# A spectral filter kernel on one core: the last matrix is loaded behind the gate's first product, with a new written-out order

## The chip, the cores and the metric

The kernel runs on one core of a Trainium2 chip. The metric is the device time of one execution in microseconds (us), the median of several runs. One execution was also recorded by the hardware profiler; all rows of the profile come from that one, and its times count from the start of its span.

## The reference

Two spectral filters act on the same input `x` (2048 rows of 1024 numbers, bf16), and a gate mixes them:

```python
g = sigmoid((x * gate_w).sum(-1, keepdims=True))      # one number a row
def filt(w_r, w_i):                                   # the same for A and for B
    X = rfft2(x.astype(float32), axes=(-2, -1))       # 2048 x 513
    return irfft2(X * (w_r + 1j * w_i), s=(2048, 1024)).astype(bfloat16)
return g * filt(A_w_r, A_w_i) + (1 - g) * filt(B_w_r, B_w_i)
```

The reference reads `A_x` for both filters. The forward transform is therefore done once.

## The kernel before, in words

All transforms are matrix products with constant matrices, in these steps.

- **Fold and S1.** `x` comes in eight loads on SyncE's (SP's) queue. VectorE folds each (`fS`, `fT`, `f2`), TensorE multiplies with the matrix F (S1), and ScalarE or VectorE evicts from PSUM (Z). A row of the gate's sum is formed on the way (`gate`, `zrow`, `zg`).
- **D and S2.** The transform along a row (D, evicted as Q) and the rest of the transform along the column (S2 and S25, evicted as X and X5), in four quarters sq = 0 to 3.
- **Products.** VectorE multiplies the spectrum with the weights of filter b (0 or 1): four products for every (b, sq), each 128x2052. The weights come in 26 pieces on GpSimd's (POOL's) queue, two transfers each.
- **I1(b, sq, th).** The first part of the inverse along the column, 16 pieces in all, each of 64 matmuls into two PSUM halves. Each half is evicted to a buffer in RING (V, on ScalarE or VectorE), and a DMA writes that buffer to other partitions of TV (the *turn*). The turn of the first half is issued by SP, that of the second by POOL. The buffer is free again when its turn has landed.
- **The gate in the inverse.** The gate's product (`gm`, half 0 and half 1) with the matrix RM and the sigmoid (`sig`) give the gate of each row. VectorE then forms RA = RM * g and RB = RM - RA (`RA`, `RB`, for each half).
- **S1A, S1B, S1H.** The second part of the inverse along the column, with RA for filter A and RB for filter B, so that the mix is made in the same sum. It is evicted as G.
- **Di.** The inverse along a row with the matrix DI, evicted as o. VectorE unfolds it (`u`, `e`, `y0`, `y1`), and SP stores it.

All matmuls are issued from one line, L392; VectorE's elementwise work from L395; evictions on ScalarE from L417 and on VectorE from L418; transfers from L426; the sigmoid from L736. In the profile's tile names R is the spectrum's buffer and later G's; WAB holds `x`, then the weights and products, and in the tail o and e; FM holds the gate and later RA; RM later holds RB.

The order of the work is not found at run time. Every step is a node with the engines that can do it, what it reads and what it writes. Three strings name the order of all 447 nodes (`ORDER`, two digits in base 36 for a node), the engine of each (`ENGS`: p, a, d, g and s for TensorE, ScalarE, VectorE, POOL and SP) and the place of each buffer in RING and PSUM (`CELLS`). Each engine runs its nodes in that order. Before a node it waits on semaphores for what the node reads, and for the last readers of what it overwrites. An engine that waits holds up everything behind it in its own list.

The list of SP in the old order is: the loads of `x` and F, the matrices DM and SK, then RM and DI, both of which wait until the last weight has landed, then SP's half of 16 turns, then nine stores. POOL has the weights and then its half of the 16 turns.

Lines that the change touches or that its steps use:

```python
    def cload(eng, t, off, key, a, b, keys, more=(), **kw):            # a constant matrix
        dma("c_" + key, eng, lambda: [(ap(t, off, [[1, b - a]]).bitcast(dt.uint16), cst[key].ap()[:, a:b])],
            (b - a) * 256e-6, 400, list(more), keys, **kw)
...
    cload("sp", RM, 0, "RM", 0, 2048, ["RM"], more=wk[1])
    cload("sp", DI, 0, "DI", 0, 2048, ["DI"], more=wk[1])
```

`more` is what the load waits for, over what its buffer needs; `wk[1]` are the weights of filter B. The buffer of DI is used for nothing else.

Of the kernel before, what the change touches and what calls it, by code (L numbers as in the profile page):

```python
# [20 lines left out]
PAIRS = {"warm": 12, "S2": 8, "I1": 64, "I1W": 32, "S25": 8, "gate": 8, "zg": 4, "gm": 8}  # L21
DEPTH = ((0, 2), (2, 4), (4, 6), (6, 8), (8, 10), (10, 12), (12, 14), (14, 16))
ORDER = (
    "020b0h030c000i04010506070m0j080n090f0a0g0d0q0s0e0o0t0r0k0y0u0p0z0w0l24150v14100x251b16111a26181g171h1c27191o1e1p1d28121r"
    "1f1q2w29131x1u1s1j2a1v2z1w1t1i2b1y1m301k1z2c2x1n1l22202d232y2132312e333v2f3z3w412g403x422h463y4a472i35434c4b36482j344d44"
    "494e2k4539624f2l4g3a643d2m4h633b3e2n4i653c3n2o3h4j373i3o3f2p4t3g383j3r4u4p2q3s3t4q3p3u2r4k3k3q5o3l2s4z4l3m535p2t504r4m5q"
    "4v544n4o4w4s5e5a5f4x6g5b516i4y665r522u2v6j6b6955676h6a566c685c6e575d6d5g7m6f5s5h6w585t7n595u6p6x5v6u5w5x6s7o6q6t6v606r6k"
    "5y7p615z6y7a6l6n806m6o7v826z7181707y7273837w7b84787x7z76748g7787757q8e858879865k8f7r5l8h7s7c7t5m5i7u8i7d5n5j7e7f8l8j7g8n"
    "8m8k8x8q8o8r7h8p8s7i7k8y8t8z7j9q7l8u9u9r909v8v9s918w9w9t9389929x94959e8a9z999y9f8c8b9a9ga5a18d9ba09ha6a99i9ca2aaa7969dab"
    "a397aoa8a49k98ak9jacapbeal9laqbfad9mamarae9nbganafba9obhatax9pbbasb1agayaubcb2ahazavbdaib3awb0biajc1bjb4bnbkc3b5c2c6b6bo"  # L30
    "c4bpblbqc5b7bsbmbrc9b8btc7bub9bwbvcbbxc8bycabzccc0cdce")
ENGS = (
    "sadsadpsasssdasdsasaspdspdapdpadpagdadpagdpadgpdadpgadpdagpdadpgadppdgapdadgdpapdgadappgdpappgapgpapgdpagpdpagpdpadpgpap"
    "dpgapdagpadpgadpagpdapgdappdpgpaddpdpgapdpagpdadpgpadpdgapddpapdadppapdapdapdassdpadadgpaspdaaspdgpadpadaspdadgpadagdasp"
    "adgspdaadsgpdaadsagpdadpdsgaadgaspdagdspdaadspaddgpaddsdadgpgspadgpspadppaspgapapdppdapadpdaddpadpdpdspapdgadpdpapdapdap"
    "ddpasdspdadpadpaddpaddpadpdadpsadpdadpadpdadpsadspdapdadapdapadpadpsaddaadsdddddddddsds")
CELLS = (
    "07150927d4002940h204097d24069024632094604620042690h460460204620460304h20614062042602355072460024206460248062424608062244"
    "0606a2804226046804202460464206402400684242000464240846c020042284044gk208402008424476508428a02")


def bf16_bits(a):
# [309 lines left out]
def bass_gated_mix__spectral_gfnet__spectral_gfnet__prompt_kernel(  # L352
# [6 lines left out]
    def sb(name, n, dty=BF):  # L359
        t = nc.alloc_sbuf_tensor(name, [128, n], dty)  # L360
        pit[id(t)] = n
        return t

    def ap(t, off, dims, p0=0, np_=128):
        return AP(t, p0 * pit[id(t)] + off, [[pit[id(t)], np_]] + [list(d) for d in dims])
# [6 lines left out]
    DI = sb("DI", 2048)  # L372
# [11 lines left out]
    P = Plan({"ps": 8, "ring": NCELL, "late": 32},  # L384
             {"ps": ("ps", 4), "p1": ("ps", 8), "st": ("ring", 4), "q": ("ring", 2), "qx": ("ring", 2), "v": ("ring", 14),
              "o": ("late", 8), "e": ("late", 8), "y": ("ring", 5), "u": ("ring", 5), "w": ("ring", 1), "dm": ("ring", 1)})
# [4 lines left out]
    def mm(o, l, r, start, stop):  # L391
        return lambda e: e.matmul(o, l, r, start=start, stop=stop, skip_group_check=True)  # L392

    def tt(o, a, b, op):
        return lambda e: e.tensor_tensor(out=o, in0=a, in1=b, op=op)  # L395
# [5 lines left out]
    def vt(n):  # L401
        return {"dve": (0.07 + 0.00052 * n, 0.205 + 0.00052 * n)}

    def pe(name, ns, build, reads, writes, alloc=(), **kw):
        return P.add(name, cost(ns), lambda e: build(), reads, writes, alloc=alloc, **kw)
# [15 lines left out]
    def dma(name, eng, pairs, mb, rate, reads, writes, kind=True, n=1, **kw):  # L421
        if not isinstance(eng, str):
            es = {"pool": (0.6, mb / 118 * 1000), "sp": (0.63, mb / 118 * 1000)}
        else:
            es = {eng: (0.6 * n, mb / rate * 1000)}
        n = P.add(name, es, lambda e: [lambda q, d=d, s=s: q.dma_start(d, s) for d, s in pairs()], reads, writes, dma=kind, **kw)  # L426
        n.mb = mb
        return n

    def psl(t, off, dims, p0=0, np_=128):  # L430
        return ap(PS, t.at * 512 + off, dims, p0, np_)
# [6 lines left out]
    def cload(eng, t, off, key, a, b, keys, more=(), **kw):  # L438
        dma("c_" + key, eng, lambda: [(ap(t, off, [[1, b - a]]).bitcast(dt.uint16), cst[key].ap()[:, a:b])],
            (b - a) * 256e-6, 400, list(more), keys, **kw)  # L440
# [30 lines left out]
    wk = {0: [], 1: []}  # L471
# [104 lines left out]
                wload("W%d%d%d" % (b, c, h), (c, 4 + h), "pool", [rows(b, c, 64 * J, 1, 8 * h, 16 * J + 8 * h, [[64 * NS, 8], [512 * NS, 4], [1, 8 * NS]]) for J in (1, 0)], 0.525, b)  # L576
                wk[b].append(("W", b, c, 4 + h))
    cload("sp", RM, 0, "RM", 0, 2048, ["RM"], more=wk[1])
    cload("sp", DI, 0, "DI", 0, 2048, ["DI"], more=wk[1])
    for c in range(4):  # L580
        gate_row(c)
    P.key = ("gate", 4)
# [145 lines left out]
    for c in range(2):  # L728
        P.key = ("gm", c)
        t = Tile("p1", 2)  # L730
        f = ap(FM, c * 1024, [[1, 1024]])
        rm = ap(RM, c * 1024, [[1, 1024]])
        pe("gm", [128] * 8, lambda c=c, t=t: [mm(psl(t, i * 128, [[1, 128]]), ap(ZG, 8 * c + i, [[0, 128]]),
                                                 ap(RM, (8 * c + i) * 128, [[1, 128]]), True, True) for i in range(8)],
           ["ZG", "RM"], [(t,)], alloc=[t])
        P.add("sig", {"act": (0.92, 1.12)}, lambda e, f=f, t=t: [lambda e: e.activation(f, psl(t, 0, [[1, 1024]]), ACT.Sigmoid)],  # L736
              [(t,)], [("gr", c)], after=[("zrow", i) for i in range(4)])
        P.add("RA", vt(1024), lambda e, f=f, rm=rm: [tt(f, rm, f, ALU.mult)], ["RM", ("gr", c)], [("RA", c)], after=[("gr", c)])
        P.add("RB", vt(1024), lambda e, f=f, rm=rm, c=c: [tt(rm, rm, f, ALU.subtract)],
              ["RM", ("RA", c)], [("RB", c)])  # L740

    for b in range(2):
        for sq in range(4):
# [136 lines left out]
```

## Time and profile before

| what | value |
|---|---|
| median of 3 runs | 122.72 us (122.67 to 123.09) |
| the profiled execution, its time | 122.33 us |
| its span, first to last instruction | 120.5 us |
| granted TensorE clock | 0.993 |
| busy: TensorE, VectorE, ScalarE, POOL | 104.1, 100.2, 96.1, 39.0 us |
| DMA: HBM read, written | 15.01 MB, 4.19 MB |

A row of a timeline or of the chain begins with its start and its duration. "x3" is three instructions merged into one row. What stands in brackets is the idle time of the engine before the row, and what ended it. PE is TensorE, PEld its weight loads, DVE VectorE, ACT ScalarE; a letter q behind an engine is its queue of issues. In a row of transfers the last number is the median time from issue to landing.

The stages, by the rows of the engines: the loads, fold and S1 run to about 22.5, D and S2 to 46, I1 with its turns from 46 to 86, and the tail (S1A to the stores) from 86 to the end, with the last I1 piece at 91.

### The profile page before, as it was taken

Reading aid. Unit: us, or ns where it says so; the run is one execution under the profiler, and the core shown is the slowest. Engines: PE = TensorE matmul, PEld = TensorE weight load, DVE = VectorE, ACT = ScalarE, POOL = GpSimd, SP = SyncE. Lnnn points to the kernel's source line nnn. Section 1 sums busy time; section 2 is a strip of 40 time slices with the busy share of each in tenths; the row PEclk is TensorE's granted clock in tenths of the full one; section 3 lists DMA queues with packets and bytes.
Section 4 is the critical chain, followed back from the end, with each engine's and each line's share of the span. In section 5 each row is a group of like instructions: output and inputs, shape, how many; then the busy total and the mean of one; then the engine's idle time right before and its main releaser. Section 6 shows DMA issues by size and latency. Waiting matters only on the chain.

```text
span 120.5 us, 4292 instructions
## 1 busy us (share of the span) xinstructions
PE 104.1 (86%) x1908; PEld 71.3 (59%) x1908; DVE 100.2 (83%) x137; ACT 96.1 (80%) x110; POOL 39.0 (32%) x72
## 2 busy tenths in 40 slices
PE   6999996899999999895997778978899999999800
PEld 2368855676974865342362334534696999999500
DVE  0459999478988999996999999784449999999991
ACT  4389999668989999957985889933578899999930
POOL 0005999999999400110311131131010100000000
PEclk9999999999999999999999999999999999999997
DMA  3999999999996883892699669979750237145384
GB/s 81 385 423 412 405 278 271 287 358 361 278 260 202 324 330 113 298 254 56 169 258 228 165 193 244 232 207 245 197 160 0 55 124 299 54 174 204 150 348 174
DMA packets 10884, 27.89 MB, mean 231 GB/s; under 512 B 3409, under 2 KB 3409, under 8 KB 10354
## 3 DMA queue, kind: packets, MB, share of 16 engines
q1 hardware_dynamic: 5472, 14.98, 37.4%
q0 software_dynamic: 5248, 12.62, 35.3%
q8 instruction: 15, 0.25, 1.0%
q10 hardware_dynamic: 146, 0.02, 0.1%
q14 instruction: 3, 0.02, 0.1%
HBM read 15.01 MB, written 4.19 MB: 159 GB/s over the span
## 4 chain that ended last, share of the span: by engine, by line
PE 37%; DMA 24%; ACT 17%; DVE 15%; issue 3%; SPq 1%; DVEq 0%; ACTq 0%
PE PS L392 37%; DMA TV<-RING 20%; DVE RING L395 12%; ACT WAB L417 6%; ACT RING L417 5%; DMA WAB<-in_A_x_dram 5%; ACT R L417 4%; DVE WAB L395 3%; DVE RING L418 1%; ACT TV L417 1%; SPq L426 1%; DVEq L251 0%; ACTq L251 0%
## 5 line engine op out<-in xcount | busy, mean ns | idle before, releaser
L417 ACT ACTIVATE RING<-PS 128x1024 bf16<-128x1024 f32 x40 | 39.1, 1028 | 12.7 <-PE PS L392 8.8
L395 DVE TENSOR_TENSOR RING<-WAB 128x1024 bf16<-128x1024 bf16 (+1 forms) x42 | 23.8, 608 | 5.3 <-DMA WAB<-in_A_x_dram 5.0
L395 DVE TENSOR_TENSOR WAB<-R,WAB 128x2052 bf16<-128x2052 bf16 x24 | 28.0, 1224 | 0.2 <-PE PS L392 0.2
L392 PE MATMUL PS<-WAB,SK 64*32 64x512 bf16 x768 | 24.4, 377 | 3.6 <-ACT RING L417 2.1
L417 ACT ACTIVATE R<-PS 128x1024 bf16<-128x1024 f32 (+2 forms) x28 | 23.7, 932 | 1.5 <-PE PS L392 1.5
L426 POOL DMA_DIRECT2D TV<-RING x16 | 8.5, 532 | 47.0 <-ACT RING L417 31.6
L392 PEld LDWEIGHTS PS<-WAB,SK 64*32 64x32 bf16 x768 | 11.0, 92 | 14.3 <-ACT RING L417 4.4
L392 PE MATMUL PS<-RING,TV 128*128 128x256 bf16 x128 | 15.1, 274 | 0.3 <-ACT TV L417 0.3
L417 ACT ACTIVATE WAB<-PS 128x1024 bf16<-128x1024 f32 (+1 forms) x17 | 14.8, 986 | 0.8 <-PE PS L392 0.7
L418 DVE CAST RING<-PS 128x1024 bf16<-128x1024 f32 x8 | 9.8, 1222 | 6.0 <-PE PS L392 3.0
L392 PEld LDWEIGHTS PS<-RING,TV 128*128 128x128 bf16 x128 | 13.5, 114 | 1.3 <-ACT R L417 0.8
L392 PE MATMUL PS<-RM,TV 128*128 128x128 bf16 x128 | 13.3, 219 | 0.5 <-DMA TV<-RING 0.5
L417 ACT ACTIVATE TV<-PS 128x1024 bf16<-128x1024 f32 x14 | 13.3, 1039 | 0.6 <-PE PS L392 0.6
L392 PE MATMUL PS<-FM,TV 128*128 128x128 bf16 x128 | 13.7, 220 | 0.0
L392 PE MATMUL PS<-DI,R 128*128 128x256 bf16 (+1 forms) x128 | 13.4, 259 | 0.2 <-ACT R L417 0.2
L392 PEld LDWEIGHTS PS<-FM,TV 128*128 128x128 bf16 x128 | 12.6, 114 | 1.3 <-DVE RING L418 0.4
L392 PE MATMUL PS<-TV,RING 128*128 128x256 bf16 (+1 forms) x128 | 12.3, 253 | 1.2 <-DVE RING L395 0.8
L392 PEld LDWEIGHTS PS<-RM,TV 128*128 128x128 bf16 x128 | 12.6, 114 | 0.7 <-DMA TV<-RING 0.7
L418 DVE CAST R<-PS 128x1024 bf16<-128x1024 f32 (+2 forms) x11 | 10.1, 935 | 3.4 <-PE PS L392 3.2
L392 PEld LDWEIGHTS PS<-TV,RING 128*128 128x128 bf16 x128 | 10.3, 98 | 4.2 <-DVE RING L395 2.2
L392 PEld LDWEIGHTS PS<-DI,R 128*128 128x128 bf16 x128 | 10.9, 98 | 1.7 <-ACT R L417 0.8
L426 POOL DMA_DIRECT2D WAB<-in_A_w_r_dram x13 | 7.8, 605 | 9.9 <-DMA WAB<-in_A_x_dram 9.9
(41 smaller groups left out, 104.1 us busy)
## 6 DMA issues: line engine op xcount, KB each, us to landing
WAB<-in_A_x_dram SPq DMA_DIRECT2D x8, 512.0 KB, 7.8
TV<-RING POOLq DMA_DIRECT2D x16, 256.0 KB, 4.2
TV<-RING SPq DMA_DIRECT2D x16, 256.0 KB, 4.6
out_dram<-RING SPq DMA_DIRECT2D x7, 512.0 KB, 2.8
WAB<-in_A_w_r_dram POOLq DMA_DIRECT2D x4, 256.5 KB, 5.9
WAB<-in_A_w_i_dram POOLq DMA_DIRECT2D x4, 256.5 KB, 6.2
WAB<-in_B_w_r_dram POOLq DMA_DIRECT2D x4, 256.5 KB, 5.3
WAB<-in_B_w_i_dram POOLq DMA_DIRECT2D x4, 256.5 KB, 5.6
```

What stands on the lines that cost most here:

```text
L392: return lambda e: e.matmul(o, l, r, start=start, stop=stop, skip_group_check=True)
L395: return lambda e: e.tensor_tensor(out=o, in0=a, in1=b, op=op)
L417: return [lambda e: e.activation(o, i, ACT.Copy)]
L418: return [lambda e: e.tensor_copy(o, i)]
L426: n = P.add(name, es, lambda e: [lambda q, d=d, s=s: q.dma_start(d, s) for d, s in pairs()], reads, writes, dma=kind, **kw)
```

## The change

The load of DI is taken from its place beside RM. It now waits for RA of half 0 instead of the weights of filter B, and stands in SP's list between its halves of turn(1,1,0) and turn(1,0,0):

```diff
     cload("sp", RM, 0, "RM", 0, 2048, ["RM"], more=wk[1])
-    cload("sp", DI, 0, "DI", 0, 2048, ["DI"], more=wk[1])
     for c in range(4):
         gate_row(c)
...
         P.add("RB", vt(1024), lambda e, f=f, rm=rm, c=c: [tt(rm, rm, f, ALU.subtract)],
               ["RM", ("RA", c)], [("RB", c)])
+    P.key = ("in", 1)
+    cload("sp", DI, 0, "DI", 0, 2048, ["DI"], more=[("RA", 0)])
```

The three strings are new as well; here are their beginnings:

```diff
 ORDER = (
-    "020b0h030c000i04010506070m0j080n090f0a0g0d0q0s0e0o0t0r0k0y0u0p0z0w0l24150v14100x251b16111a26181g171h1c27191o1e1p1d28121r"
+    "020b0h030c000i04010506070m0j080n090f0a0g0d0q0e0s0o0r0t0k0y0u0p0z0w0l0v241510140x251b18111a12261h19161g13271o1c171j281e1i"
...
 ENGS = (
-    "sadsadpsasssdasdsasaspdspdapdpadpagdadpagdpadgpdadpgadpdagpdadpgadppdgapdadgdpapdgadappgdpappgapgpapgdpagpdpagpdpadpgpap"
+    "sadsadpsasssdasdsasaspsdpadpdpadpaagdpdagdpadgpdapdagpdadgpdadpgadppdagpdadpgapddagpdpapgadpappgpgpapgdpagpdpagpdpapgadp"
...
```

Decoded, the lists differ in this way. Of the I1 pieces, with the engines of their two evictions (A ScalarE, D VectorE), first half before second:

```
old: 010 AA, 011 AD, gm 0, 000 AA, 021 AA, 001 AA, 020 AA, 030 AA, 111 AA, 031 AA, 120 AA, 110 AA, gm 1,
     100 AD, 130 DA, 131 DA, S1A, 101 AD, S1A, S1B ..., 121 AD
new: 010 AA, 011 DA, gm 0, 000 AA, 020 AA, 021 AA, 001 AA, 030 AA, 031 AA, 111 AA, 120 AA, 110 AA, gm 1,
     100 AA, 130 AA, S1A, 131 AD, 101 AA, S1A, S1B ..., 121 AA
```

- Evictions that change engine: 31. ScalarE has 116 nodes instead of 111, VectorE 132 instead of 137.
- The first turn: the old order evicts the second half of V(0,1,0) first, the new one the first half.
- VectorE's last products are followed by RA and RB of half 0 and then of half 1 in the new order; in the old one by RA of half 1, RA of half 0, RB of half 1, RB of half 0.
- In the forward stage the third gate row and its eviction stand ahead of the last S1 pieces (in the old order the eviction stands behind the last Z). The order of the pieces of D and S2 and some of their evictions' engines change.
- Buffers: in the old order an eviction V takes the buffer of the V that stands about five places ahead of it; in the new one five to seven places in the middle and four near V(1,0,0) and V(1,3,0).
- In the tail the pieces 9 to 13 of S1H, G, Di and o come in another order, and so do the stores. The second G of the tail is evicted by VectorE instead of ScalarE, and both evictions of the last I1 piece by ScalarE.

Weights, matrices, matmuls and transfers are the same in number, shape and size.

More of the change, by code (lines that the diff above doesn't have):

```diff
@@ L23 @@
 ORDER = (
-    "020b0h030c000i04010506070m0j080n090f0a0g0d0q0s0e0o0t0r0k0y0u0p0z0w0l24150v14100x251b16111a26181g171h1c27191o1e1p1d28121r"
-    "1f1q2w29131x1u1s1j2a1v2z1w1t1i2b1y1m301k1z2c2x1n1l22202d232y2132312e333v2f3z3w412g403x422h463y4a472i35434c4b36482j344d44"
-    "494e2k4539624f2l4g3a643d2m4h633b3e2n4i653c3n2o3h4j373i3o3f2p4t3g383j3r4u4p2q3s3t4q3p3u2r4k3k3q5o3l2s4z4l3m535p2t504r4m5q"
-    "4v544n4o4w4s5e5a5f4x6g5b516i4y665r522u2v6j6b6955676h6a566c685c6e575d6d5g7m6f5s5h6w585t7n595u6p6x5v6u5w5x6s7o6q6t6v606r6k"
@@ L28 @@
[L28 to L31, printed above, removed]
+    "020b0h030c000i04010506070m0j080n090f0a0g0d0q0e0s0o0r0t0k0y0u0p0z0w0l0v241510140x251b18111a12261h19161g13271o1c171j281e1i"
@@ new lines @@
+    "1d1p2y291f1w1k1m1q1l2a2v1r2z1x1u2b1n1s1z1y1t2c311v222w202d32232x2130332e3y2f3u3z402g3v3w412h453x49462i344a4b35382j4c4243"
+    "39472k443e48623c2l3f4h643d2m3a634i2n3q3b363m3g3r3h2o3n3o3j374f653i2p3p3k4d5o3l4g2q3s4e4y5p2r3t4j4z2s4o4k4s4p522t4t4q4l5q"
+    "534m4u4n4r4v595d5a4w6g5e506i4x666h512u6j6b67545r6968556e6a5b6c565c6f5f6w6d5s5g7m575t6x585u6k7n5v6u5w6p6l7o6n6m6v6s6o5x82"
+    "6q6t6r6y80605y83615z7p7371816z7276707v7874778g7579847y7w8h7z857x7q7a87868e885j7b7t7r8f7u7c5k7s5h5n5i8i7d5l7f5m7e8x8l7g8j"
@@ L32 @@
+    "8m8n8k8o8q8p7h8r8s7k8y8t7i7l9u8u8z7j9q9v909r8v919s8w9w9t9289939x95949e8c9z99969f8a9y8d9a97a99ga08ba59b98aa9ha1a69c9iab9d"
+    "a7a2ac9jax9ka3a8b19ma4ayaoadae9lb2beagapaz9nafbfb3b0bab49obgbbb59pakb6bhahbcalb7aqaibdb8amajarbjb9bnbianc1bkboatbpbqasc2"
+    "bsbrblc4c3aubmc5c6buavbtc7c8awbwc9cbcabvccbxcdbycebzc0")
 ENGS = (
-    "sadsadpsasssdasdsasaspdspdapdpadpagdadpagdpadgpdadpgadpdagpdadpgadppdgapdadgdpapdgadappgdpappgapgpapgdpagpdpagpdpadpgpap"
-    "dpgapdagpadpgadpagpdapgdappdpgpaddpdpgapdpagpdadpgpadpdgapddpapdadppapdapdapdassdpadadgpaspdaaspdgpadpadaspdadgpadagdasp"
@@ L35 @@
-    "adgspdaadsgpdaadsagpdadpdsgaadgaspdagdspdaadspaddgpaddsdadgpgspadgpspadppaspgapapdppdapadpdaddpadpdpdspapdgadpdpapdapdap"
-    "ddpasdspdadpadpaddpaddpadpdadpsadpdadpadpdadpsadspdapdadapdapadpadpsaddaadsdddddddddsds")
+    "sadsadpsasssdasdsasaspsdpadpdpadpaagdpdagdpadpgdapdagdpadgpdadpgadppdagpdadpgapddagpdpapgadpappgpgpapgdpagpdpagpdpapgadp"
+    "dpgapadpgapdagpdagpappddpgapddpdagappdaagpapdgapdgpapdpgapddappaadppapdapdapdasdpaddaspagpdaagpdspadpadaspdadgpadasdagpd"
+    "agspdaadgsdpadagaspdagdsdpaadgaspdasdgpdaadgpasdsdpadadspagagpsadspgpappagpdaspdpapdpapadpdaddpadpdpadgpdpadspdsapdapdpa"
@@ L37 @@
+    "pdadpddapdsapdddapdapddapdpadpadspdadpadpdadpsadspdapdadapdapadpadsapddaadsdddddddddsds")
 CELLS = (
-    "07150927d4002940h204097d24069024632094604620042690h460460204620460304h20614062042602355072460024206460248062424608062244"
-    "0606a2804226046804202460464206402400684242000464240846c020042284044gk208402008424476508428a02")
+    "07150927d4002940h2d4007924h602074260294024702h07402409240700274062h40620506420460202355672042006224460068242a06406248062"
+    "4a240062460240462268a026022046002404680242606040286424002c664008286042c0440208408476c50072846")
```

## The prediction

> **What bounds the kernel now.** I read the page first, then the chain of work that ended last, then busy time by stretches, and then each engine's timeline around the two places that the change touches. Times are microseconds from the start of the span. I call a piece of the inverse I1(b,q,t), its two evictions V(b,q,t) and their two transfers turn(b,q,t), as the kernel does.
>
> ```profile
> span 120.5 us, 4292 instructions
> PE 104.1 (86%) x1908; PEld 71.3 (59%) x1908; DVE 100.2 (83%) x137; ACT 96.1 (80%) x110; POOL 39.0 (32%) x72
> GB/s 81 385 423 412 405 278 271 287 358 361 278 260 202 324 330 113 298 254 56 169 258 228 165 193 244 232 207 245 197 160 0 55 124 299 54 174 204 150 348 174
> PE 37%; DMA 24%; ACT 17%; DVE 15%; issue 3%; SPq 1%; DVEq 0%; ACTq 0%
> ```
>
> Three engines are above 80%, and the chain changes hands between four resources. So no single sum over the span decides; each stage has its own limit.
>
> ```profile
> 22.50:46.00 23.50, 23.43 (x288) 17.39 (x296) 19.42 (x25) 20.53 (x24) 18.07 (x32) 1.00 0.88 291
> 50.00:54.00 4.00, 3.26 (x84) 1.55 (x88) 4.00 (x5) 2.89 (x4) 0.56 (x1) 1.00 0.96 233
> 54.00:57.00 3.00, 1.58 (x48) 0.69 (x56) 2.07 (x3) 2.11 (x3) 0.00 (x0) 1.00 0.24 65
> 70.00:75.00 5.00, 4.11 (x136) 2.01 (x120) 5.00 (x5) 4.30 (x5) 1.49 (x3) 1.00 0.85 217
> 75.00:78.00 3.00, 2.70 (x96) 1.35 (x104) 2.25 (x4) 2.78 (x4) 0.53 (x1) 1.00 1.03 243
> 78.00:82.00 4.00, 3.18 (x109) 1.46 (x94) 3.17 (x5) 1.47 (x3) 1.04 (x2) 1.00 0.78 195
> 99.50:118.00 18.50, 14.65 (x195) 13.14 (x193) 18.27 (x38) 16.12 (x22) 0.00 (x0) 1.00 0.50 200
> ```
>
> The columns are the stretch and its length, busy PE, PEld, DVE, ACT and POOL, the granted clock, the DMA share and GB/s. TensorE fills the forward stage (23.43 of 23.50). VectorE fills 50 to 54, 70 to 75 and the tail. The DMA engines are full at 50 to 54 and 75 to 78, with a hole between (0.24 in 54 to 57), in which TensorE and ScalarE idle too.
>
> ```profile
> 49.25 5.55 DMA TV<-RING
> 61.12 5.43 DMA TV<-RING
> 67.89 3.24 DMA TV<-RING
> 75.27 4.83 DMA TV<-RING
> 81.44 4.50 DMA TV<-RING
> 85.99 10.84 PE PS L392 x200
> ```
>
> These are the turns on the chain: start, time to landing. An eviction can't write a buffer until the turn that reads it has landed, so between 48 and 86 the end runs eviction, turn, eviction. After 86 TensorE leads, then ScalarE and VectorE.
>
> **The inverse matrix leaves its early place.**
>
> ```profile
> 46.04 0.32 SPq L426 DMA_DIRECT2D RM<-c_RM  x1
> 46.41 0.43 SPq L426 DMA_DIRECT2D DI<-c_DI  x1
> RM<-c_RM SPq DMA_DIRECT2D x1, 512.0 KB, 5.4
> DI<-c_DI SPq DMA_DIRECT2D x1, 512.0 KB, 7.2
> TV<-RING POOLq DMA_DIRECT2D x16, 256.0 KB, 4.2
> TV<-RING SPq DMA_DIRECT2D x16, 256.0 KB, 4.6
> 54.89 1.02 ACT L417 ACTIVATE RING<-PS 128x1024 bf16<-128x1024 f32 x1 [1.70 <-DMA TV<-RING]
> 47.93 2.85 ACT L417 ACTIVATE RING<-PS 128x1024 bf16<-128x1024 f32 x3 [0.29 <-PE PS L392]
> 52.95 1.05 PE L392 MATMUL PS<-WAB,SK 64*32 64x512 bf16 x32
> ```
>
> DI lands 7.2 after its issue at 46.41, at 53.6, and lies over the first turn, which takes 5.55 and lands at 54.80. ScalarE idles 1.70 for it and starts V(0,0,0) at 54.89. With DI gone I give the first turn the median of the SP queue, 4.6: the new order evicts its SP half first (47.93 + 1.02), it is issued 0.3 later as now, at 49.25, and lands at 53.85. I1(0,0,0) ends at 52.95 + 1.05 = 54.0 at the latest, so V(0,0,0) starts at 53.9 instead of 54.89: **1.0 gained**. The ends are nothing (RM alone crowds it as much) and the whole 1.70.
>
> The Trainium skill (DMA: Bandwidth & Descriptors, Anatomy of one DMA — SWDGE (gpsimd) path) gives a transfer 2.0 us and its bytes at 436 GB/s, which is 2.6 us for a turn, an estimate; by it all 1.70 would go and the sum below would be 1.6 gained instead of 0.9. The trace does not agree, with 3.24 to 5.55 on its chain, and the measurement decides.
>
> **The forward stage and its new order.** Up to the first I1 nothing is added or removed. TensorE has 0.07 free in 22.5 to 46, so the order can gain nothing there.
>
> ```profile
> 21.33 1.02 ACT L417 ACTIVATE TV<-PS 128x1024 bf16<-128x1024 f32 x1 [0.18 <-PE PS L392]
> 22.25 0.59 ACT L417 ACTIVATE FM<-PS 128x512 bf16<-128x512 f32 x1
> ```
>
> It can lose: a gate row's eviction (0.59, now behind the last eviction of the first transform) moves ahead of it. ScalarE idles 0.18 there, and TensorE does the gate's product earlier too and has it off its list later. I take 0, with ends 0.1 gained and 0.6 lost. Some evictions change places between VectorE and ScalarE, each of which idles over 2.9 in that stretch.
>
> **Does the early gain last to 75?** VectorE multiplies through this stage.
>
> ```profile
> 56.86 1.23 DVE L395 TENSOR_TENSOR TV<-R,WAB 128x2052 bf16<-128x2052 bf16 x1 [0.93 <-ACT R L417]
> 58.01 11.48 DVE L395 TENSOR_TENSOR WAB<-R,WAB 128x2052 bf16<-128x2052 bf16 x10
> 69.64 5.79 DVE L395 TENSOR_TENSOR WAB<-R,WAB 128x2052 bf16<-128x2052 bf16 x5 [0.15 <-PE PS L392]
> 76.19 1.29 DVE L395 TENSOR_TENSOR FM<-RM,FM 128x1024 bf16<-128x1024 bf16 x2 [0.75 <-ACT FM L736]
> ```
>
> The 0.93 at 56.86 waits for the eviction that stands on ScalarE behind V(0,0,0). One us earlier there closes this hole, and the products then run back to back at (11.48 - 1.23) / 9 = 1.14 each; the last one ends at 74.5 instead of 69.64 + 5.79 = 75.4. So VectorE lets 0.9 through and little more (0.93 + 0.15 are all its idle time). The turns must keep pace as well. Counted in the lists, the eviction that reuses a buffer stands on average five places behind the one that filled it in the old order, and six from the 13th to the 21st eviction in the new one. That is room for the middle. I carry **0.9**, and count no more of it as gain.
>
> **The inverse matrix at its new place.** DI waits for RA of half 0, which needs only a gate that is long evicted, so it comes right behind the last product: issue at about 75.3, behind turn(1,1,0) (75.27 on the chain, some 0.9 sooner then) and ahead of SP's half of turn(1,0,0). Queued behind the wait on SP are turn(1,0,0), (1,3,0), (1,3,1), (1,0,1), (1,2,1) and all stores; POOL's halves pass it by. The issue itself costs SP 0.43, which nothing there feels. Its 524 KB at the highest rate of the page, 423 GB/s, take the DMA engines 1.24. Turn(1,0,0) is the one held; its reader is S1B at 85.99, which in any case waits until 85.94 for turn(1,3,0) (81.44 + 4.50), issued behind it. The part that can hurt is the sharing with turn(1,1,0), whose landing releases V(1,3,0). It is issued over 0.5 ahead on the same queue. I take **0.2 lost**; the ends are 0 and 2.5 (1.24 on each of two turns that follow one another on the chain).
>
> ```profile
> L392 PEld LDWEIGHTS PS<-DI,R x128: 96/98/99, 88.7 to 113.9; 128*128 128x128 bf16 x128
> ```
>
> DI is first read at 88.7. With its old 7.2 it lands at 82.5. That cover is 6 us; without it TensorE would stand at the first Di2.
>
> **The last evictions and the tail.**
>
> ```profile
> 85.71 1.23 DVE L418 CAST RING<-PS 128x1024 bf16<-128x1024 f32 x1 [2.61 <-DMA TV<-RING]
> 86.66 2.85 ACT L417 ACTIVATE R<-PS 128x1024 bf16<-128x1024 f32 x3 [0.69 <-PE PS L392]
> 88.90 1.22 DVE L418 CAST R<-PS 128x1024 bf16<-128x1024 f32 x1 [1.96 <-PE PS L392]
> ```
>
> The new order gives both evictions of I1(1,0,1) to ScalarE, ahead of the first G, where VectorE took one: (2.85 - 1.02) / 2 = 0.92 more on ScalarE, of which some 0.5 lie behind the landing of turn(1,3,0). In return the second G goes to VectorE, which idles 1.96 before 88.90, so the third is out 0.9 sooner. From there on both orders give VectorE five evictions and ScalarE loses one; VectorE has 0.23 free from 99.5 to 118. I take **0.2 gained**, between 0.9 either way (one eviction's worth).
>
> **Sum.** -0.9 for the early place, +0.2 for the new one, -0.2 for the tail: -0.9. The profiled execution took 122.33 (span 120.5 and 1.8 around it), so 121.4; the median of the runs is 122.72, 0.39 above it, so **121.8**. The case's own range, with 0 to 1.7 for the first term, is 121.2 to 122.4.
>
> **The rivals.**
>
> *More comes through.* TensorE has holes in the late pieces that end with an eviction that itself waited for a turn.
>
> ```profile
> 72.22 1.93 PE L392 MATMUL PS<-WAB,SK 64*32 64x512 bf16 x64 [0.59 <-ACT RING L417]
> 79.88 1.93 PE L392 MATMUL PS<-WAB,SK 64*32 64x512 bf16 x64 [0.82 <-DVE RING L418]
> ```
>
> If six places of room close these two, 1.4 more: 120.4. For it speaks that one turn on the chain took only 3.24. Against it, the new order's last reuses, before V(1,0,0)'s second half and V(1,3,0), are back at four places.
>
> *Moved, not saved.* The DMA engines give back at 75 what they gained at 47: then the new place costs 1.24 instead of 0.2, and the sum is +0.1, 122.8. For it speaks the share of 1.03 in 75 to 78, higher than the 0.96 of the old place. The same time comes out if the change does not do what it says, because RM and four turns in a row crowd each other without DI.
> The Trainium skill (DMA: Bandwidth & Descriptors, Issuing engines are not separate DMA queues) says that transfers from every issuing engine share the same 16 DMA engines and interleave; this is that rival's rule, and the full shares while both queues are in use agree.
>
> *Slower: a tight loop in front of the matrix.* In the new order V(1,1,0), turn, V(1,3,0), turn, S1B is a chain with four places of room, all on ScalarE's queue in order, and DI falls between the two turns. If both are held by 1.24, the new place costs 2.5, and the sum is +1.4: 124.1. It decides once turn(1,1,0) lands later than 81.4, since 80.10 (75.27 + 4.83) is its landing now and the 0.9 won early, with the tail's 0.2, is then spent. Against it, the share falls to 0.78 in 78 to 82, where the second turn would run.
>
> **How the numbers follow.** Forecast 0.42, more 0.12, moved 0.18, slower 0.28. About 0.5% (0.6 us) is what a measurement of this kernel can tell from no change. Faster by more: three quarters of the forecast's range, nearly all of the first rival and a sliver of the second, 0.45. Slower by more: nearly all of the third rival and the edges of the others, 0.30. The rest, 0.25. The range takes in both ends, 120.3 to 124.1, and leaves out half of the first rival and about a third of the last.
>
> **What would show it.** Right: the first turns land under 5 us and V(0,0,0) starts near 53.9; VectorE's wait of 0.93 is gone and the last product ends near 74.5; DI is issued near 75 and lands before 83; S1B starts near 85. The forecast is wrong if the first turns still take 5.5, if a new wait appears before a product on VectorE, if turn(1,1,0) or turn(1,3,0) takes over 6, or if S1B starts early and the end does not, which would put the fault in the tail.

## The result, and the profile after

The kernel after takes 122.68 us (median of 20 runs, 121.4 to 124.92), the kernel before 121.88 us beside it (20 runs, 120.77 to 123.21). The ratio is 1.0061, with an interval of 1.0035 to 1.0087: slower by 0.6%, where the forecast was 0.9 us faster. The time lies inside the forecast's range of 120.3 to 124.1; its direction is the other one. Ratios here leave out executions more than 1.5% above the fastest of their kernel, so they need not be the ratio of the medians; the profiles of old_order_late, old_order_late_free, new_order_late_free and new_order_half are of such executions, and no price of a change is taken from them.

The profiled execution took 122.99 us. Its page and its chain of work, as far as they answer to the lines shown of before:

```profile
span 121.2 us, 4292 instructions
DMA 32%; POOL 24%; PE 15%; DVE 15%; ACT 7%; issue 3%; SPq 1%; DVEq 0%
...
46.03 5.27 DMA RM<-c_RM
...
60.73 4.97 DMA TV<-RING
...
70.11 4.04 DMA TV<-RING
...
75.23 4.86 DMA TV<-RING
...
81.16 5.59 DMA TV<-RING
...
86.79 11.73 PE PS L392 x216
```

DMA's share of the chain went from 24% to 32%, but not by the turns: theirs fell from 19.5% to 16.1%. Ahead of 51 the chain after runs through POOL's issues of the weights, the last weight and RM (24.3%, 5.0% and 4.3%), where before it ran through VectorE and TensorE. The chain before had TensorE from 85.99 (S1B); now it has it from 86.79. The engines' timelines around the two places, and the row of DI among the transfers:

```profile
53.97 1.02 ACT L417 ACTIVATE RING<-PS 128x1024 bf16<-128x1024 f32 x1 [0.87 <-PE PS L392]
57.42 17.18 DVE L395 TENSOR_TENSOR WAB<-R,WAB 128x2052 bf16<-128x2052 bf16 x15
74.18 1.02 ACT L417 ACTIVATE RING<-PS 128x1024 bf16<-128x1024 f32 x1 [0.27 <-DMA TV<-RING]
75.80 1.57 SPq L426 DMA_DIRECT2D DI<-c_DI  x1
DI<-c_DI SPq DMA_DIRECT2D x1, 512.0 KB, 7.1
TV<-RING SPq DMA_DIRECT2D x16, 256.0 KB, 4.4
80.11 1.93 PE L392 MATMUL PS<-WAB,SK 64*32 64x512 bf16 x64 [1.45 <-ACT RING L417]
86.79 1.08 PE L392 MATMUL PS<-RM,TV 128*128 128x128 bf16 x16 [1.10 <-DMA TV<-RING]
```

What the prediction asked for up to 75 is there: V(0,0,0) starts at 53.97, the products run without a hole and end at 57.42 + 17.18 = 74.60. But V(1,1,0) starts at 74.18, where before had it at 74.22 by its timeline, and from there every step is late. So there are two questions: where the early microsecond went, and what the late load costs.

### The profile page after: what moved, and what is told of

The parts are those of the page before. It is cut to its first block, busy times and chain, and to the rows that moved or that the text cites. A ratio compares the mean times of both kernels' runs of the same rounds, so it can differ in the third digit from the quotient of the medians.

```text
span 121.2 us, 4292 instructions
## 1 busy us (share of the span) xinstructions
PE 104.8 (86%) x1908; PEld 70.4 (58%) x1908; DVE 98.0 (81%) x132; ACT 98.0 (81%) x115; POOL 39.0 (32%) x72
## 4 chain that ended last, share of the span: by engine, by line
DMA 32%; POOL 24%; PE 15%; DVE 15%; ACT 7%; issue 3%; SPq 1%; DVEq 0%
POOL WAB L426 24%; DMA TV<-RING 16%; PE PS L392 15%; DVE RING L395 7%; ACT RING L417 7%; DMA WAB<-in_A_x_dram 6%; DVE WAB L395 6%; DMA WAB<-in_B_w_i_dram 5%; DMA RM<-c_RM 4%; DVE WAB L418 2%; SPq L426 1%; DVEq L251 0%
## 5 line engine op out<-in xcount | busy, mean ns | idle before, releaser
L417 ACT ACTIVATE RING<-PS 128x1024 bf16<-128x1024 f32 x42 | 41.2, 1029 | 11.4 <-PE PS L392 8.3
L417 ACT ACTIVATE R<-PS 128x1024 bf16<-128x1024 f32 (+3 forms) x32 | 25.7, 863 | 2.1 <-PE PS L392 2.1
L418 DVE CAST RING<-PS 128x1024 bf16<-128x1024 f32 x6 | 7.3, 1223 | 8.1 <-PE PS L392 8.1
L417 ACT ACTIVATE WAB<-PS 128x1024 bf16<-128x1024 f32 (+1 forms) x15 | 13.1, 955 | 0.7 <-PE PS L392 0.6
L418 DVE CAST R<-PS 128x1024 bf16<-128x1024 f32 x7 | 8.5, 1222 | 5.4 <-PE PS L392 5.4
```

What stands on the lines that cost most here:

```text
L417: return [lambda e: e.activation(o, i, ACT.Copy)]
L418: return [lambda e: e.tensor_copy(o, i)]
```

## The experiments

All kernels but those with "free" in the name use the buffers of the kernel whose order they have. "Old" and "new" order are the orders of before and after; "early" is DI's place beside RM, "late" its place behind RA. Two explanations stood against each other: the late place costs what the order wins, or the new order itself wins nothing or loses. The expectations say in place which theory gives which number. The strings change only where DI's node has another place or number, unless it is said otherwise.

**One part at a time.** new_order_early is the kernel after with DI put back beside RM; old_order_late is the kernel before with DI alone moved.

```diff
 new_order_early (against after)
-    cload("sp", DI, 0, "DI", 0, 2048, ["DI"], more=[("RA", 0)])
+    cload("sp", DI, 0, "DI", 0, 2048, ["DI"], more=wk[1])
 old_order_late (against before)
-    cload("sp", DI, 0, "DI", 0, 2048, ["DI"], more=wk[1])
...
+    cload("sp", DI, 0, "DI", 0, 2048, ["DI"], more=[("RA", 0)])
```

> The new order with the load of DI put back beside RM, ahead of the first turn. Theory P (the late place is what costs: DI stretches the last turns, turn(1,3,0) from 4.5 to 5.6, and the order by itself is even): V(0,0,0) goes back to about 54.9, turn(1,3,0) to about 4.5, S1B to about 86, and the time to that of the kernel before, within 0.3 us. Theory O (the new order itself is slower, because the late evictions reuse buffers at four places): S1B stays at 86.8 or later and the time is 0.7 to 1.5 us above the kernel before.

> The old order with DI alone moved: it waits for RA of half 0 and stands on SP between turn(1,1,0) and turn(1,0,0). Theory P: the first turns land sooner as in the changed kernel (V(0,0,0) near 53.9), the late turns are stretched by about 1.1, S1B comes out within 0.4 of 86.4 and the time is 0 to 0.7 us above the kernel before. Theory O: the early gain comes through, S1B near 85.2 and the time 0.5 to 0.9 us below the kernel before.

Measured: new_order_early 0.9988 (0.9948 to 1.0029), old_order_late 1.0244 (1.0182 to 1.0306) against before. The new order by itself, its tail included, is not to be told from the old one, and the late place costs 0.7% in the new order (1.0061 - 0.9988; by the two intervals 0.2 to 1.2%) and 2.4% in the old. Neither theory had the 2.4%: theirs were at most 0.7 us, and it is about 3. Three stretches (75 to 78, 78 to 81, 81 to 84) of after, and then of new_order_early; the columns are those of the prediction's stretches:

```profile
75.00:78.00 3.00, 2.71 (x101) 1.08 (x80) 2.28 (x4) 2.40 (x4) 0.00 (x0) 1.00 0.90 223
78.00:81.00 3.00, 1.55 (x50) 0.98 (x50) 0.00 (x0) 2.57 (x3) 1.06 (x2) 1.00 0.99 281
81.00:84.00 3.00, 1.85 (x72) 0.84 (x64) 1.23 (x1) 1.16 (x2) 0.36 (x1) 1.00 0.95 229
```

```profile
75.00:78.00 3.00, 1.87 (x80) 0.80 (x64) 2.05 (x4) 3.00 (x4) 0.00 (x0) 1.00 0.75 207
78.00:81.00 3.00, 2.42 (x81) 1.25 (x72) 0.23 (x1) 2.55 (x3) 1.06 (x2) 1.00 0.66 181
81.00:84.00 3.00, 1.85 (x72) 0.84 (x64) 1.23 (x1) 1.02 (x1) 0.53 (x1) 1.00 0.67 198
```

The DMA share is the last number but one. With DI there are (0.15 + 0.33 + 0.28) x 3 = 2.28 us more of all DMA engines in these nine; what DI's own packets take of it and what others take longer beside them is not parted here. TensorE loses 0.87 in the second stretch, but had gained 0.84 in the first, where V(1,1,0) came earlier in the kernel after (74.18 against 74.84). From new_order_early's transfers, its ScalarE timeline, TensorE's and VectorE's, set against after:

```profile
TV<-RING SPq DMA_DIRECT2D x16, 256.0 KB, 3.5
53.96 1.02 ACT L417 ACTIVATE RING<-PS 128x1024 bf16<-128x1024 f32 x1 [0.88 <-PE PS L392]
85.31 1.06 PE L392 MATMUL PS<-RM,TV 128*128 128x128 bf16 x16
57.43 17.18 DVE L395 TENSOR_TENSOR WAB<-R,WAB 128x2052 bf16<-128x2052 bf16 x15
```

SP's turns have a median of 3.5 instead of 4.4, and S1B starts at 85.31 without a wait instead of 86.79 behind a wait of 1.10 for a turn. The 1.48 us between them are those of two single executions: new_order_none below, without any DI, has S1B at 86.15. The price is told by time, 0.7%. Up to the last product both kernels agree to 0.01 us (53.96 and 53.97, 57.43 and 57.42), although one has DI beside RM and the other has not.

What agrees from execution to execution are the two turns between V(1,1,0) and S1B. SP's transfers issued in the windows of turn(1,1,0) and turn(1,3,0), first of new_order_early, then of new_order_none (below), both with the new order and without DI under way there:

```profile
TV<-RING SPq DMA_DIRECT2D x1, 256.0 KB, 3.4
TV<-RING SPq DMA_DIRECT2D x1, 256.0 KB, 4.1
TV<-RING SPq DMA_DIRECT2D x1, 256.0 KB, 3.2
TV<-RING SPq DMA_DIRECT2D x1, 256.0 KB, 3.7
```

In the kernel after they take 4.86 and 5.59, by its chain: both are held, each by about 1.5. It is not DI's place in SP's list that holds them: turn(1,0,0), the one behind DI, is issued at 77.42 in the kernel after and at 77.72 in new_order_early. But S1B loses less than the sum of both, since the steps behind the turns had some room without DI: in new_order_early turn(1,1,0) landed at 79.31 and V(1,3,0) came at 79.75, turn(1,3,0) landed at 84.93 and S1B came at 85.31.

In the old order the same load does more harm. The chain of old_order_late, its TensorE timeline, and two stretches:

```profile
77.65 7.14 DMA TV<-RING
85.95 3.21 PE L392 MATMUL PS<-WAB,SK 64*32 64x512 bf16 x64 [4.17 <-ACT RING L417]
84.00:87.00 3.00, 1.05 (x32) 0.61 (x40) 0.23 (x1) 1.02 (x1) 0.53 (x1) 0.91 0.59 167
87.00:90.00 3.00, 3.00 (x55) 1.50 (x35) 0.79 (x1) 0.79 (x1) 0.00 (x0) 0.53 0.33 87
```

The turn at 77.65 takes 7.14; the eviction on the chain that follows it is V(1,3,1), which in the old order takes the buffer of the V four places ahead of it. TensorE stands for 4.17 and then does a piece in 3.21 instead of 1.93, at a granted clock of 0.53. In the new order V(1,3,1) reuses buffers filled nine and eleven places earlier, and no such wait appears in the kernel after.

**Is there anything to win at the early place?** Both orders without DI's load; Di reads RM's buffer in place of DI, so the last product is with another matrix and the output is not that of the filters.

```diff
 old_order_none (new_order_none leaves out the load behind RA)
-    cload("sp", DI, 0, "DI", 0, 2048, ["DI"], more=wk[1])
...
-                            f.append(mm(psl(t, hh * 128, [[1, 128]]), l, ap(DI, w, [[1, 128]]), True, True))
+                            f.append(mm(psl(t, hh * 128, [[1, 128]]), l, ap(RM, w, [[1, 128]]), True, True))
...
-                    pe("Di", [256] * 4, lambda c=c, t=t: di(c, t), [("G", n2, c), "DI"], [(t,)], alloc=[t])
+                    pe("Di", [256] * 4, lambda c=c, t=t: di(c, t), [("G", n2, c), ("RB", 0), ("RB", 1)], [(t,)], alloc=[t])
```

> The new order without any load of DI; the last products read RM (by then RB) instead, so the output is not the reference's. Theory P: turn(1,3,0) is back at about 4.5, S1B at about 85.5, the time 1.1 us below the changed kernel and 0.4 below the kernel before. Theory O: the late turns don't gain by it, the time is at most 0.3 us below the changed kernel.

> The old order without any load of DI, the last products reading RM as in the run beside it. Theory P: the early gain alone, V(0,0,0) near 53.9, with nothing paid later: 0.5 to 1.0 us below the kernel before, and no more than 0.5 below the new order without DI. Theory O: the same early gain, 0.9 us below the kernel before, and 1 us or more below the new order without DI.

Measured: 1.0016 (0.9975 to 1.0057) and 0.9999 (0.9959 to 1.0040). With half a megabyte less to load there is nothing to be seen: at its early place DI costs no more than 0.4% in either order. So both theories missed in the old order, where each had 0.5 us or more gained, and Theory P missed in the new one, where it had 0.4. Two more looks at the kernel before ask whether its first turn is always late:

```diff
 (before_b, before_c: no edit)
```

> The kernel before, unchanged, for a second profile of it. If the first turn's 5.55 us and V(0,0,0) at 54.89 are DI's doing, they come again, within 0.3. If they were one execution's accident, the first turn lands at 53 to 54.2 and V(0,0,0) starts at 53.5 to 54.3 with DI in its early place.

> The kernel before, unchanged, for a third profile; the same two readings as in the run beside it.

They took 121.29 and 122.4 us. ScalarE's row of V(0,0,0), VectorE's first rows of ten or more products, and the stretch 54.5 to 58, of before_b and then of before_c; the last fence has that stretch of the profiled before:

```profile
53.50 1.02 ACT L417 ACTIVATE RING<-PS 128x1024 bf16<-128x1024 f32 x1 [0.83 <-PE PS L392]
56.98 17.18 DVE L395 TENSOR_TENSOR WAB<-R,WAB 128x2052 bf16<-128x2052 bf16 x15
54.50:58.00 3.50, 2.95 (x100) 1.52 (x108) 3.50 (x4) 2.44 (x4) 0.53 (x1) 1.00 0.45 112
```

```profile
53.64 1.02 ACT L417 ACTIVATE RING<-PS 128x1024 bf16<-128x1024 f32 x1 [0.83 <-PE PS L392]
57.11 11.65 DVE L395 TENSOR_TENSOR WAB<-R,WAB 128x2052 bf16<-128x2052 bf16 x10
54.50:58.00 3.50, 2.81 (x97) 1.43 (x105) 3.50 (x4) 2.44 (x4) 0.53 (x1) 1.00 0.45 111
```

```profile
54.50:58.00 3.50, 2.08 (x76) 1.00 (x80) 2.57 (x3) 2.89 (x4) 0.00 (x0) 1.00 0.30 71
```

With DI still beside RM, V(0,0,0) starts at 53.50 and 53.64, earlier than in the kernel after (53.97), and it waits for TensorE's I1(0,0,0), not for a turn. So it does in every other profile of this case, with DI there or not. VectorE fills 3.50 of 3.50 there; its hole of 0.93 is in the one execution only. The wait of 1.70 on which the forecast was built is no property of the kernel.

DI does hold the first turn all the same. The first turn of before_b and of old_order_none, then of new_order_early and of after:

```profile
TV<-RING POOLq DMA_DIRECT2D x1, 256.0 KB, 3.9
TV<-RING POOLq DMA_DIRECT2D x1, 256.0 KB, 3.0
TV<-RING SPq DMA_DIRECT2D x1, 256.0 KB, 4.4
TV<-RING SPq DMA_DIRECT2D x1, 256.0 KB, 3.1
```

It takes 3.0 and 3.1 without DI beside it and 3.9 and 4.4 with it (3.5 in before_c), but it has always landed before I1(0,0,0) ends. Only in the profiled before, with 5.55, did it come later.

**Does the reuse of buffers carry the delay?** RING has cells that are free from the middle of the kernel on; these four kernels give each V of that stage a cell that no pending turn reads. Only the string of cells differs (and DI's place, as above).

```diff
 CELLS (old_order_free; one piece)
-    ...h20614062042602355072460024206460248062424608062244"
+    ...h206140620426p2r5t032460c24e0690624p06rt2424g06i24k"
```

> The kernel before with other places for the 32 buffers of V: each takes the cells of RING that have lain unused longest (32 cells instead of the first 12), so that an eviction never waits for a recent turn. Theory R (the evictions wait for turns only because the order reuses buffers too soon): ScalarE's and VectorE's waits for turns go, the I1 stage is bound by the products, whose last ends at 74 to 75.4 as before, S1B starts at 83 to 84 and the time falls by 1.5 to 2.5 us. Rival D (the DMA engines are the bound): the turns are issued sooner and take longer to land, 6 us or more, S1B stays within 0.5 of 85.5 and the time within 0.5 us of the kernel before.

> The new order with DI beside RM, with the same free placing of the V buffers. Theory R: 1.5 to 2.5 us below the same order with its own buffers, as for the old order, so that the two orders come out within 0.5 us of one another. Rival D: within 0.5 us of the run without free buffers.

> The old order with DI moved behind RA, which took 3 us more than before with its own buffers, now with the free placing. Theory R (most of the 3 us came because V(1,3,1) and V(1,0,1) reuse the buffers of the turns that DI holds up): what is left is one stretched turn ahead of S1B, and the time is 0.8 to 1.5 us above old_order_free, not 3. Rival D: DI costs its 3 us with these buffers too.

> The changed kernel with the free placing alone. Theory R: DI's late place costs about 1 us over new_order_early_free (one stretched turn ahead of S1B), whatever the order. Rival D: 0.7 us as with its own buffers, and no gain over the changed kernel beyond 0.5 us.

Measured: old_order_free 0.9879 (0.9797 to 0.9961), new_order_early_free 0.9888 (0.9840 to 0.9935), old_order_late_free 0.9974 (0.9923 to 1.0025), new_order_late_free 1.0032 (0.9990 to 1.0073). Groups of evictions on ScalarE (the last part is its idle time and what ended it), in the old order of before_b and old_order_free:

```profile
L417 ACT ACTIVATE RING<-PS 128x1024 bf16<-128x1024 f32 x40 | 39.1, 1028 | 12.1 <-PE PS L392 8.2 <-DMA TV<-RING 3.9
```

```profile
L417 ACT ACTIVATE RING<-PS 128x1024 bf16<-128x1024 f32 x40 | 38.8, 1030 | 12.5 <-PE PS L392 12.5
```

And in the new order of new_order_early and new_order_early_free:

```profile
L417 ACT ACTIVATE RING<-PS 128x1024 bf16<-128x1024 f32 x42 | 40.8, 1029 | 11.0 <-PE PS L392 8.7 <-DMA TV<-RING 2.3
L417 ACT ACTIVATE RING<-PS 128x1024 bf16<-128x1024 f32 x42 | 40.5, 1029 | 9.8 <-PE PS L392 9.8
```

The 3.9 and 2.3 us in which evictions waited for turns are gone, and 1.1 to 1.2% of the time with them, in both orders alike. So both kernels with free buffers and DI in its early place beat before and after; new_order_early_free takes 120.41 us (median of 12 runs). No more came than the lower end of the 1.5 to 2.5 us expected, and less than the waits' size: in the rows ScalarE waits longer for TensorE instead (12.5 against 8.2, 9.8 against 8.7). With free buffers the late DI still costs about 0.9% in the old order (0.9974 - 0.9879; by the intervals 0 to 1.9%) and 1.4% in the new (1.0032 - 0.9888; 0.8 to 2.1%). In the old order the price fell from 2.4%, so there the reuse carried part of it, by the middle values most; in the new it did not fall. What takes its place is not shown by time; in both profiles it is S1B that waits for a turn, 2.17 in the new order and 3.08 in the old.

**Another place, and half of it.** new_order_later puts DI three turns further down SP's list, behind SP's half of turn(1,3,1), and so behind the turns that lead to S1B; new_order_half loads half of the matrix at each place.

```diff
 new_order_half
-    cload("sp", DI, 0, "DI", 0, 2048, ["DI"], more=[("RA", 0)])
+    cload("sp", DI, 1024, "DI", 1024, 2048, ["DI"], more=[("RA", 0)])
+    cload("sp", DI, 0, "DI", 0, 1024, ["DIa"], more=wk[1])
 new_order_later: only the position of DI's node in ORDER and ENGS
```

> The changed kernel with DI one place further on: behind SP's half of turn(1,3,1), the last turn that S1B does not need at once. Theory P (DI stretches the turns that stand beside and behind it, and of those S1B waits for turn(1,3,0)): turn(1,3,0) is back at 4.1 to 4.6 and S1B starts at 85.3 to 85.8; DI lands near 89, where the first Di wants it at 89.5; the time is within 0.4 us of new_order_early, 0.7 below the changed kernel. Rival W (waiting for a late DI, or its wait on SP, is what costs): TensorE waits for DI at the first Di2 and the time is that of the changed kernel or above.

> The changed kernel with DI in two halves: one beside RM, early, and one at the late place. Theory P (the price is the DMA time of the bytes that are loaded there): turn(1,3,0) takes about 4.8 to 5.0, the time is about halfway, 0.3 to 0.5 us above the kernel before's order with DI early. Rival W: the wait on RA and the place on SP cost the same for half the bytes, and the time is that of the changed kernel.

Measured: new_order_later 1.0173 (1.0112 to 1.0233), new_order_half 1.0011 (0.9975 to 1.0046). The half is between the two ends, as a price by bytes would have it, but its interval takes in the one (0.9988) and overlaps with that of the other (1.0035 to 1.0087), so it decides little. The later place is told by TensorE's timeline, the chain and one stretch:

```profile
84.83 1.06 PE L392 MATMUL PS<-RM,TV 128*128 128x128 bf16 x16
83.05 6.44 DMA DI<-c_DI
89.62 4.45 PE L392 MATMUL PS<-DI,R 128*128 128x128 bf16 x32 [1.95 <-DMA DI<-c_DI]
89.62:94.00 4.38, 4.38 (x32) 3.59 (x32) 2.05 (x4) 1.66 (x2) 0.00 (x0) 0.61 0.07 22
```

Out of the way of the turns that lead to S1B, DI lets S1B start at 84.83, 1.96 before the kernel after and 0.48 before new_order_early; the two turns took 3.4 and 4.2. That confirms who pays at 75: the turns of the loop. The turns now under way with DI are held instead, 5.6 and 5.5 for the two issued at 85.81 and 86.46, against 3.5 for the same two in new_order_early. And now DI itself is late: the first Di2 stands 1.95 for it and, at a granted clock of 0.61 over its stretch, takes 4.45. The theory that the time would be within 0.4 us of new_order_early had left that out; its rival had it. In new_order_early the same 32 matmuls take 2.80:

```profile
87.99 2.80 PE L392 MATMUL PS<-DI,R 128*128 128x128 bf16 x32
```

## Why the prediction was wrong, step by step

- **The early place: predicted 1.0 gained, in fact nothing.** The step that failed is the first: a wait of 1.70 behind a turn of 5.55 was taken from one execution as the kernel's own. In two others, unchanged, the first turn is not what V(0,0,0) waits for, and I1(0,0,0) is. The prediction had that bound ("at the latest 54.0"), but used it only as the end of the gain. The kernels without DI gain nothing, which shows it by time.
- **What was right in that step, and why it did not help.** Without DI the first turn did become short, 3.1 where 4.6 was forecast, and V(0,0,0) did start near 53.9 (53.97). But with DI beside RM it starts there too (53.96 in new_order_early). The lower end of the term, nothing, was the true one, though not for the reason given with it, that RM alone crowds the turn as much.
- **The forward stage and its new order: predicted 0, with ends of 0.1 gained and 0.6 lost.** By the rows it lost 0.2 to 0.4: the first V evictions begin at 48.28 in the kernel after, against 47.93, 47.91 and 48.05 in the three executions of before. By time the order as a whole is even (0.9988).
- **Does it last to 75?** VectorE's part came as said: no hole, the last product at 74.60 for a predicted 74.5. But with the old order and the old place before_b ends its products at 56.98 + 17.18 = 74.16 and before_c at 74.88, so this was no gain over the kernel before. And the sentence that the turns must keep pace was passed over with a count of places. In the kernel after, V(1,1,0) waits until 74.18 for a turn whose chain runs from 60.73 (4.97) over 70.11 (4.04).
- **The new place: predicted 0.2 lost, in fact 0.7% or 0.9 us by time.** This is the term that was mis-sized and turns the sign. Three things were off. DI's time on the DMA engines was taken at the page's best rate, 1.24; in the stretches where it runs they moved 223 to 281 GB/s and were busy for 2.28 more. The delay was put on turn(1,0,0) alone; in fact turn(1,1,0) and turn(1,3,0), which stand one behind the other on the chain, were both held, to 4.86 and 5.59 from 3.2 to 3.4 and 3.7 to 4.2 in the same order without DI there. And the share of 0.78 in 78 to 82, which spoke for a free stretch, was that of the old order without DI there; with DI it is 0.99 and 0.95. The upper end of the term, 2.5, held all of it.
- **DI's cover.** It was issued at 75.80, not 75.3, landed 7.1 later, near 83, and Di did not wait. This was right, and new_order_later shows the cost once the cover of 6 us is used up.
- **The tail: predicted 0.2 gained, measured about 0.1.** From S1B to VectorE's last row it takes 31.90 after (86.79 to 118.69) and 32.02 before (85.99 to 118.01). It is steady: 31.87 in new_order_early, 32.02 and 32.03 in before_b and before_c. The last rows of VectorE, of after and then of before:

```profile
117.48 1.21 DVE L395 TENSOR_TENSOR RING<-WAB 128x512 bf16<-128x512 bf16 x3
```

```profile
116.80 1.21 DVE L395 TENSOR_TENSOR RING<-WAB 128x512 bf16<-128x512 bf16 x3
```

- **The rivals.** "Slower: a tight loop in front of the matrix" named the right loop, the right sign and the right mechanism: both turns of the loop are held, by about 1.5 each where it had 1.24. What it had wrong is its condition: turn(1,1,0) landed at 75.23 + 4.86 = 80.09, well before 81.4, and the time was lost all the same. That landing is the one of before (80.10), for the new order alone shortens this turn to 3.4 and DI takes that back. Its 2.5 was too much, since V(1,3,0) and S1B had room for part of it. "Moved, not saved" came nearest in size: its price for the new place was 1.24, and without the first term's gain its sum would be +1.0. That the measured 122.68 lies by its 122.8 is luck: 122.8 was counted from a kernel before of 122.72, which measured 121.88 beside the kernel after. The rule of the Trainium skill named with it (DMA: Bandwidth & Descriptors, Issuing engines are not separate DMA queues) agrees with the stretches from 75 to 84: half of the turns come from POOL's queue, DI from SP's, and all share the engines' time.
- **The range.** "0 to 1.7 for the first term" does not give 121.2 to 122.4: with the other two terms it gives 122.7 and, if all of it came through, 121.0.
- **The signs of being wrong.** None of those named came: the first turn took 3.1, no product waited, the two turns stayed under 6. Only S1B near 85 failed, at 86.79. The signs asked for one turn over 6, and two turns of about 5 in a row were enough.

In sum, by the times: nothing is gained at the first place (instead of 0.9), 0.1 by the order with its tail (0.9988, which can't be told from nothing; instead of 0.2), and 0.9 is lost at the new place (instead of 0.2). That gives +0.8, and +0.8 is measured (122.68 - 121.88). It has to, since the 0.9 is itself a difference of two of these times; what shows the cause is that only DI's place differs between the two kernels.

## What to carry to other kernels

Before a term of a sum rests on one long wait, ask what would be waited for a moment later, and look at a second execution: the first turn took 5.55, 3.94 and 3.51 in three executions of one kernel, and the wait behind it was there in one. Price a load in the stretch where it will run, at the rate that the engines reach there and with the transfers that it stretches, and not by its bytes at the best rate of the page. A slack place for a load is one where the transfers that it stretches still land before anyone on the chain waits for them: here the early place was free, though the first turn was stretched there too, and freeing the buffers that make evictions wait for turns was worth more than any place of the load.

## What the runs showed of the hardware

- After a stand of TensorE of about 2 us or more the granted clock can fall to about half. In old_order_late an idle time of 4.17 is followed by 0.53 in the stretch from 87; in new_order_later 1.95 by 0.61 over 4.38. In three more profiles stands of 2.17, 2.36 and 3.08 are followed by 0.66, 0.57 and 0.55 over the next 3.4 to 4.1 us (new_order_late_free, new_order_half, old_order_late_free). But 2.11 in new_order_early_free left it at 1.00, as the rows below show, and so did stands of 1.45 and 1.10 in the kernel after (1.00 in 81 to 84 and in 87 to 90). So the length of the stand alone does not decide it. Where it falls, a late transfer is paid twice: 1.3 more for one piece (3.21 against 1.93), 1.65 more for the first Di2 (4.45 against 2.80). All five kernels with the fall load DI, or half of it, late. The Trainium skill (TensorE: Matmul & The Clock Gate, Part 1: The HAM clock gate) has the gate fall to half rate after about 3.4 us of idling; the 4.17 agrees, and the four shorter stands do not, so the measurement decides.

```profile
73.53 3.66 PE L392 MATMUL PS<-WAB,SK 64*32 64x512 bf16 x128 [2.11 <-DVE WAB L395]
73.50:77.00 3.50, 3.48 (x128) 2.04 (x128) 3.43 (x5) 1.86 (x3) 0.00 (x0) 1.00 0.72 195
```

- SP was held 1.57 by DI's issue in the kernel after, and 0.43 by the same issue at the early place; the issue in new_order_later, in the row below, took 0.59, and in old_order_late, at the place of the kernel after, 0.34. So the 1.57 is not a price of the place.

```profile
83.05 0.59 SPq L426 DMA_DIRECT2D DI<-c_DI  x1
```

- The same kernel's span was 119.5 and 120.5 in two executions on one chip (before_b, before_c). Differences of 0.5% are told by many timed runs, not by the rows of one profile.
